# A fused WKV attention and mixture-of-experts kernel: fixed places for expert 0's weight parts, another order of loads and tables in the head, finer routing steps in the transition

## The chip, the core and the metric

The kernel runs on one NeuronCore of a Trainium2 chip. The core has TensorE (PE; its weight loads are listed as PEld), VectorE (DVE), ScalarE (ACT), GpSimd (POOL) and SyncE (SP, which here only issues DMAs). Each engine works through its own instructions in the order in which they were written, and semaphores make it wait for the others. The metric is the device time of one execution in microseconds.

## What is computed

Two layers follow one another. The first is a linear attention (WKV) over `r, k, v` of shape (4, 8, 768, 48), with one decay `w` and one bonus `u` per head and dimension:

```python
for t in range(S):
    kt, vt, rt = (k[:, :, t], v[:, :, t], r[:, :, t])
    cur = np.einsum('bhd,bhe->bhde', u[None] * kt, vt)
    y[:, :, t] = np.einsum('bhd,bhde->bhe', rt, state + cur)
    state = w[None, :, :, None] * state + np.einsum('bhd,bhe->bhde', kt, vt)
```

Its output, as 3072 tokens of 384 numbers, goes into a mixture of eight experts with a noisy top-2 router:

```python
logits = x @ w_gate
noisy_logits = logits + np.log1p(np.exp(x @ w_noise)) * noise
top2 = np.argpartition(-noisy_logits, 2, axis=1)[:, :2]
# softmax over the two, then for each expert e and each of its tokens:
h = np.maximum(x[mask] @ w1[e], 0.0)      # 384 -> 1024
out[mask] += top2_w[mask, k, None] * (h @ w2[e])   # 1024 -> 384
```

All inputs and the output are float32. The expert products are made from two fp32r parts of each operand, a high part and the low rest, with three matmuls for one (high by high, high by low, low by high).

## The kernel before

The schedule is written out by hand: the order of the Python calls is the order of each engine's instructions.

**Head.** SP issues the loads of the first chunks of `k`, `r`, `v`, then `u`, the gate's weights and the noise. DVE and ACT build tables of powers of the decay: `pwk` and `pwr` (lines 160 to 177), `w128` (line 179). PE turns `pwk` around, and ACT copies the result into `tabk` (line 194), by which every later chunk of `k` is multiplied on POOL (`prep_k`, line 307). POOL also makes the products `r*k*u` (`uterm_a`, lines 314 and 316); `uterm_b` sums them on DVE and scales `v` by them (`cv`).

**Attention.** 24 chunks of 128 tokens (`NT`; six time steps for each of four batches). Iteration i of the loop transposes chunk i+1 (`trans`), turns chunk i-1's output for the gate (`xtrans`), updates the state (`zup`: DVE `zt`, ACT `z` and `zb`), makes `cv` of chunk i+1 (`uterm_b`, on DVE up to chunk 8, on ACT in eight pieces from chunk 9 on), computes the output of chunk i on PE (`yout`) and adds `cv` on DVE (`xout`, `x`, line 404), makes the gate's logits of chunk i-1, then the scores of chunk i+1 (`scores`, PE, line 346), which DVE masks (`mask`, `am`, line 354). The next `yout` needs `am`, and the next `xtrans` needs `x`.

**Routing.** After 8, 16 and 24 chunks a group of chunks is routed: some ninety small DVE instructions and a few PE matmuls into one PSUM bank (`RT`), written as the generator `route`. `rstep(us)` takes as many of its pieces as a credit in microseconds allows, at three places of each iteration. When a piece ends with PE work, `at_pe` and `gap` hold that work back for `gap` calls. `drop` turns slots into lists (one-hot products `r_oa`, `r_ob` on DVE, lines 510 to 519, then eight matmuls, line 523).

**Expert weights.** An expert has seven weight units (three of `w1`, four of `w2`, named `w0h/w0l` and `w1h/w1l` on chip). Each unit is a generator: SP loads it into one of three staging buffers (`stg`, line 276), then after `NLAG` empty steps ACT copies the high part (line 279), then DVE subtracts it for the low part (line 281). `wstep()` moves every running unit by one step and starts the next when fewer than three run. Expert 0's units run inside the attention loop, before `yout`, by two `wstep` calls in each iteration from 2 to 10 and one afterwards.

**Transition.** Expert 0's tokens come in three chunks, (0,0), (0,1), (0,2), of two, two and two and a half tiles. `p1` makes the hidden layer: 8 groups f of 9 matmuls, ACT and DVE write the two parts `hb` (and `ht` for the half tile), with three PSUM buffers in turn. `p2` makes the output: 24 matmuls for each tile. While these run, DVE finishes group 2's routing and the lists for all experts (`rest`, by `rest_step`), POOL gathers rows (`xg`), `xT` turns them (PE `ptm`, ACT `xh`, DVE `xl`), and expert 1's weights are split. From chunk (1,0) on the work is the same for each expert.

## Time and profile before

| | |
|---|---|
| Median of 3 runs | 660.09 us (659.82 to 660.27) |
| The profiled execution | 659.12 us, its span 657.4 us |
| PE busy | 626.2 us (95%) |
| DVE busy | 349.4 us (53%) |
| ACT busy | 262.7 us (40%) |
| POOL busy | 262.9 us (40%) |
| HBM read and written | 59.03 MB and 19.76 MB |

A row of a timeline gives start, duration, engine, source line, operation, tiles and a count; in brackets stands the idle time of that engine just before, and what ended it. Times are microseconds from the start of the span. Matmuls overlap one another in the pipeline, so PE is idle only where no matmul is under way. In the rows of a window, each engine's busy time is followed by its count of instructions; PEclk is the share of full TensorE speed that was granted.

### The profile page before, as it was taken

How to read it: one execution, taken by the hardware profiler on the slowest of the kernel's cores; microseconds unless marked ns; L12 is line 12 of the kernel's file. 1: busy time of each engine (PE TensorE's matmuls, PEld its weight loads, DVE VectorE, ACT ScalarE, POOL GpSimd, SP SyncE). 2: the span in 40 equal slices, each digit the busy share in tenths (PEclk: the TensorE clock that was granted, in tenths of full speed). 3: DMA queues.
4: the chain of work that ended last, by engine and by line, in shares of the span. 5: the costliest groups of instructions: out<-in, count | busy, mean ns of one | idle time of the engine just before them, and what ended most of it. 6: DMA issues, size and time to landing. Idle time of an engine off the chain costs nothing.

```text
span 657.4 us, 11894 instructions
## 1 busy us (share of the span) xinstructions
PE 626.2 (95%) x4436; PEld 595.4 (91%) x4437; DVE 349.4 (53%) x883; ACT 262.7 (40%) x737; POOL 262.9 (40%) x389
## 2 busy tenths in 40 slices
PE   7999889999997889999999999999999999999993
PEld 4998789998897879999999999999999999999993
DVE  8786778797479935253452525345252534523230
ACT  1566656775323424243251524325152433523210
POOL 8775526453101247313631641363174136315211
PEclk9999979999999999999999999999999999999997
DMA  8997667773204535242533434253343425302101
GB/s 128 233 227 175 133 142 164 162 174 101 81 1 153 184 118 167 90 133 74 182 107 104 152 98 134 71 183 100 111 153 96 132 72 181 95 26 86 37 2 37
DMA packets 111444, 78.87 MB, mean 120 GB/s; under 512 B 86721, under 2 KB 101441, under 8 KB 111378
## 3 DMA queue, kind: packets, MB, share of 16 engines
q1 hardware_dynamic: 101442, 49.19, 30.2%
q0 software_dynamic: 9936, 28.83, 14.0%
q8 instruction: 37, 0.61, 0.4%
q14 instruction: 29, 0.24, 0.1%
HBM read 59.03 MB, written 19.76 MB: 120 GB/s over the span
## 4 chain that ended last, share of the span: by engine, by line
PE 83%; DVE 11%; ACT 2%; issue 2%; DMA 0%; POOL 0%; POOLq 0%; DVEq 0%; SPq 0%
PE ph L857 31%; PE pym L891 30%; PE py L396 5%; PE pa L346 3%; PE ptm L832 3%; DVE am L354 2%; PE pl L426 2%; PE py L388 2%; PE pym L884 2%; PE pt L334 2%; PE pym L882 2%; PE pwarm L364 1%; DVE RT L454 1%; PE ptx L414 1%; ACT cv L327 1%
## 5 line engine op out<-in xcount | busy, mean ns | idle before, releaser
L891 PE MATMUL pym<-w1h,hb 128*128 128x384 f32 x768 | 204.2, 339 | 0.0
L912 POOL DMA_INDIRECT out_dram<-ot,TK x56 | 57.6, 1029 | 219.9 <-DVE ot L908 200.6
L857 PE MATMUL ph<-xh,w0h 128*128 128x384 f32 (+3 forms) x408 | 142.3, 349 | 1.7 <-ACT xh L833 1.7
L891 PEld LDWEIGHTS pym<-w1h,hb 128*128 128x128 f32 x768 | 139.4, 188 | 1.1 <-issue 0.3
L857 PE MATMUL ph<-xl,w0h 128*128 128x384 f32 (+3 forms) x408 | 139.6, 342 | 0.5 <-DVE xl L834 0.2
L857 PE MATMUL ph<-xh,w0l 128*128 128x384 f32 (+3 forms) x408 | 139.4, 342 | 0.0
L861 DVE SCALAR_TENSOR_TENSOR hb<-ph,hb 128x384 fp32r<-128x384 f32 (+1 forms) x136 | 72.4, 532 | 113.9 <-ACT ht L859 68.4
L891 PE MATMUL pym<-w1l,hb 128*128 128x384 f32 x384 | 129.3, 337 | 0.0
L859 ACT ACTIVATE hb<-ph 128x384 fp32r<-128x384 f32 (+1 forms) x136 | 64.3, 473 | 120.0 <-PE ph L857 112.4
L897 ACT ACTIVATE ot<-pym 128x384 f32<-128x384 f32 x45 | 22.1, 492 | 160.4 <-PE pym L891 155.8
L805 POOL DMA_INDIRECT xg<-xd,GR x56 | 54.0, 964 | 80.1 <-DVE f L687 35.1
L857 PEld LDWEIGHTS ph<-xh,w0h 128*128 128x128 f32 x408 | 77.1, 189 | 5.1 <-ACT xh L833 2.4
L857 PEld LDWEIGHTS ph<-xl,w0h 128*128 128x128 f32 x408 | 77.1, 189 | 3.7 <-DVE xl L834 1.2
L857 PEld LDWEIGHTS ph<-xh,w0l 128*128 128x128 f32 x408 | 77.2, 189 | 2.6
L891 PEld LDWEIGHTS pym<-w1l,hb 128*128 128x128 f32 x384 | 72.2, 188 | 0.1
L834 DVE TENSOR_TENSOR xl<-ptm,xh 128x384 fp32r<-128x384 f32 (+1 forms) x56 | 28.9, 524 | 74.3 <-ACT xh L833 63.3
L814 POOL DMA_INDIRECT pv<-out_dram,GA x49 | 55.6, 1134 | 25.9 <-issue 14.9
L396 PE MATMUL py<-vt,am 128*128 128x96 f32 x384 | 60.8, 284 | 2.9 <-DVE am L354 2.0
L396 PEld LDWEIGHTS py<-vt,am 128*128 128x128 f32 x384 | 52.0, 197 | 5.1 <-DVE am L354 4.8
L307 POOL TENSOR_TENSOR kd<-kt,tabk 128x192 f32<-128x192 f32 x46 | 27.4, 617 | 57.8 <-PE pwarm L364 50.6
L281 DVE TENSOR_TENSOR w1l<-stg,w1h 128x768 fp32r<-128x768 f32 x32 | 30.8, 961 | 10.2 <-ACT w1h L279 10.2
L354 DVE TENSOR_TENSOR am<-pa,mneg 128x512 int32<-128x512 int32 x48 | 30.7, 680 | 8.8 <-PE pa L346 6.9
(205 smaller groups left out, 865.8 us busy)
## 6 DMA issues: line engine op xcount, KB each, us to landing
stg<-in_moe_w_dram SPq DMA_DIRECT2D x24, 512.0 KB, 4.2
stg<-in_moe_w_dram SPq DMA_DIRECT2D x32, 384.0 KB, 3.3
rd<-in_r_dram SPq DMA_DIRECT2D x24, 192.0 KB, 4.5
vt<-in_v_dram SPq DMA_DIRECT2D x24, 192.0 KB, 4.1
xd<-x SPq DMA_DIRECT2D x24, 192.0 KB, 2.0
out_dram<-zrow SPq DMA_DIRECT2D x16, 288.0 KB, 3.7
kt<-in_k_dram SPq DMA_DIRECT2D x23, 192.0 KB, 3.3
xg<-xd,GR POOLq DMA_INDIRECT x56
```

The lines of the kernel that those rows point to most:

```text
L281: nc.vector.tensor_sub(lo, tv, hi.bitcast(F32))
L307: (eng or nc.gpsimd).tensor_mul(kd[i % 3][:, h, :D], kt[i][:, h], tabk[:, h, :D])
L354: nc.vector.tensor_tensor(am[:, s].bitcast(I32), pa[s].bitcast(I32), mneg.to_broadcast([128, NP, 128]), op=ALU.bitwise_and)
L396: nc.tensor.matmul(o2, AM[i][:, s, p, :], vt[i][:, h, None, :].to_broadcast([128, 2, D]), start=not c and h == 0, stop=h == H - 1, skip_gr ...
L805: nc.gpsimd.indirect_dma_start(out=xg[:n], out_offset=None, in_=xd[:GROUPS[GEARLY - 1][1] * 128] if early_ else xd, in_offset=bass.Indirec ...
L814: nc.gpsimd.indirect_dma_start(out=pv[:n], out_offset=None, in_=out, in_offset=bass.IndirectOffsetOnAxis(ap=GA[:n, e * NJ + t:e * NJ + t + ...
L834: nc.vector.tensor_sub(xl[:, :, o:o + n], pt[:, :, :n], xh[:, :, o:o + n].bitcast(F32))
L857: nc.tensor.matmul(ph[:, :w_], a[:, d, fs], x[:, d, :w_], start=(j == 0), stop=(j == len(q) - 1))
L859: nc.scalar.activation(h_[:, f, 0, :], ph[:, a:b], AF.Relu)
L861: nc.vector.scalar_tensor_tensor(h_[:, f, 1, :], ph[:, a:b], 0.0, h_[:, f, 0, :].bitcast(F32), op0=ALU.max, op1=ALU.subtract)
L891: nc.tensor.matmul(py, hb[:, f, a, hs], x[:, f, :], start=(j == 0), stop=(j == len(q) - 1))
L912: st = nc.gpsimd.indirect_dma_start(out=out, out_offset=bass.IndirectOffsetOnAxis(ap=TK[:n, q:q + 1], axis=0), in_=ot[:n], in_offset=None, ...
```

## The change

Three groups of edits.

**Expert 0's weights.** `wstep` leaves the attention loop. Three tables say in which iteration each of the seven units is loaded (`W_LD`), copied (`W_HI`) and subtracted (`W_LO`). The copy stays where `wstep` was; the subtraction and the load go to the end of the iteration, behind `mask` and `kvup`. Units 5 and 6 wait in their staging buffers for iterations 21 and 22.

**Head.** Chunk 1's `k` and chunk 0's `v` are loaded ahead of `u`, chunk 1's `r` after them. Half of `pwr` is copied by ACT rather than DVE, `w128` is made after the first transposed tiles. POOL prepares chunk 1 of `k` before chunk 0's products. DVE's preparation of chunk 0 (`prep_k(0)`, `uterm_b(0)`) goes behind the transposes of chunk 1, thus behind `rT` of chunk 1.

**Transition.** Routing steps run between the matmuls of `p2(0,0)`, at every eighth, with a third of the credit. `gap` stays 2 in the rest of the lists, with slightly larger credits. Expert 1's weight steps are left out of `p1(0,2)` and doubled in `p1(1,0)`. The first tile of chunk (1,0) is turned inside `p2(0,2)`, one tile ahead.

```diff
+W_LD = {1: (0,), 2: (1, 2), 4: (3,), 5: (4,), 6: (5,), 7: (6,)}
+W_HI = {4: (0,), 5: (1,), 6: (2,), 7: (3,), 8: (4,), 21: (5,), 22: (6,)}
+W_LO = {4: (0,), 5: (1,), 6: (2,), 7: (3,), 8: (4,), 22: (5,)}
...
     load(0, (0, 2))
+    load(1, (0, 1))
+    load(0, (2, 3))
+    load(1, (1, 2))
     ub = const.tile([128, H, D], F32, name="ub")
     nc.sync.dma_start(ub, ...)
-    load(0, (2, 3))
-    load(1)
+    load(1, (2, 3))
...
-    nc.vector.tensor_copy(pwr[:, :, 0:64], pwk[:, :, 127:63:-1])
+    nc.scalar.activation(pwr[:, :, 0:64], pwk[:, :, 127:63:-1], AF.Copy)
...
-    NLAG = [4]
+    NLAG = [1]
...
-    wq.extend(w_split(0))
+    wun = w_split(0)
     consts_a()
+    prep_k(1)
     uterm_a(0)
-    prep_k(1)
     uterm_a(1)
     consts_b()
     scores(0)
     mask(0)
-    prep_k(0, nc.vector)
-    uterm_b(0)
...
             trans(i + 1)
+        if i == 0:
+            prep_k(0, nc.vector)
+            uterm_b(0)
...
-        for _ in range(0 if i < 2 else 2 if i < 11 else 1):
-            wstep()
+        for p in W_HI.get(i, ()):
+            next(wun[p])
...
         kvup(i)
         rstep(STEPS_KV)
+        for p in W_LO.get(i, ()) + W_LD.get(i, ()):
+            next(wun[p])
...
-    while wq or wrun:
-        wstep()
+    next(wun[6])
...
-    for t in p2(0, 0):
-        rstep(STEPS_P2)
+    for t in p2(0, 0, lambda: rstep(STEPS_P2 / 3)):
...
-    gap[0] = 1
-    for t in p2(0, 1, lambda: rest_step(1.0)):
+    for t in p2(0, 1, lambda: rest_step(1.2)):
...
             if s == 2:
-                rest_step(STEPS_P1)
-            elif XT_AT <= j < XT_AT + 2:
+                rest_step(1.1)
+                continue
+            if XT_AT <= j < XT_AT + 2:
                 next(xt, None)
             wstep()
+            if s == 3:
+                wstep()
...
-            if s > 2:
+            if s > 2 or listed[0] and t > chunks(e)[ci][0]:
                 next(xt, None)
```

Where instructions move, three places matter. The first is DVE around the attention's iteration 8, where group 0's routing begins (`x` and `am` belong to the loop, `w1l` is a weight's low part, the rest is routing). Before:

```order
L321 TENSOR_REDUCE c_979<-rku 128x8
L281 TENSOR_TENSOR w1l_720<-stg,w1h_719 128x768 x2
L404 TENSOR_TENSOR x<-py,cv 128x384
L354 TENSOR_TENSOR am<-pa,mneg 128x512 x2
L565 SCALAR_TENSOR_TENSOR RT<-lg 128x64
L567 TENSOR_SCALAR r_a<-RT 128x64
```

Now:

```order
L327 TENSOR_REDUCE c_980<-rku 128x8
L410 TENSOR_TENSOR x<-py,cv 128x384
L360 TENSOR_TENSOR am<-pa,mneg 128x512 x2
L571 SCALAR_TENSOR_TENSOR RT<-lg 128x64
L573 TENSOR_SCALAR r_a<-RT 128x64
L574 SCALAR_TENSOR_TENSOR RT<-lg,nz 128x64
L448 TENSOR_SCALAR RT<-r_a 128x64
L450 TENSOR_SCALAR RT<-RT 128x64
L578 TENSOR_TENSOR r_zp<-RT,lg 128x64
L287 TENSOR_TENSOR w1l_673<-stg,w1h_672 128x768
L345 TENSOR_TENSOR rT<-pt,pwr 128x512
```

The two low parts ahead of `x` are gone from there; one comes behind `am` and the first routing pieces, ahead of the next `rT`.

The second place is DVE in `p1(0,2)`, between the first and the last list of group 2 (`hb` and `ht` empty PE's hidden groups, `r_oa` and `r_ob` are what PE's list matmuls wait for). Before:

```order
L514 TENSOR_TENSOR r_ob<-r_ej,ij 128x8x49
L281 TENSOR_TENSOR w1l_3181<-stg,w1h_3180 128x768
L861 SCALAR_TENSOR_TENSOR hb<-ph,hb 128x256
L861 SCALAR_TENSOR_TENSOR ht<-ph,ht 128x64
L517 TENSOR_TENSOR r_ob<-r_ob,thi 128x8x49
L281 TENSOR_TENSOR w1l_3181<-stg,w1h_3180 128x768
L861 SCALAR_TENSOR_TENSOR hb<-ph,hb 128x256
L861 SCALAR_TENSOR_TENSOR ht<-ph,ht 128x64
L519 TENSOR_SCALAR r_ob<-r_ob,pcol 128x8x49
```

Now:

```order
L520 TENSOR_TENSOR r_ob<-r_ej,ij 128x8x49
L523 TENSOR_TENSOR r_ob<-r_ob,thi 128x8x49
L867 SCALAR_TENSOR_TENSOR hb<-ph,hb 128x256
L867 SCALAR_TENSOR_TENSOR ht<-ph,ht 128x64
L525 TENSOR_SCALAR r_ob<-r_ob,pcol 128x8x49
```

The weight parts between the pieces of `r_ob` have left; they come in `p2(0,2)` and `p1(1,0)`.

The third place is ACT from the end of `p2(0,2)` into `p1(1,0)`, where expert 1's and expert 2's high parts are copied. Before:

```order
L886 ACTIVATE ot<-pym 64x384
L833 ACTIVATE xh<-ptm 128x3x128
L835 ACTIVATE GT<-xg 128x1
L833 ACTIVATE xh<-ptm 128x3x128
L835 ACTIVATE GT<-xg 128x1
L833 ACTIVATE xh<-ptm 128x3x128
L835 ACTIVATE GT<-xg 128x1
L859 ACTIVATE hb<-ph 128x384 x4
L279 ACTIVATE w0h_3550<-stg 128x1024
L859 ACTIVATE hb<-ph 128x384
```

Now:

```order
L892 ACTIVATE ot<-pym 64x384
L839 ACTIVATE xh<-ptm 128x3x128
L841 ACTIVATE GT<-xg 128x1
L285 ACTIVATE w1h_3180<-stg 128x768
L839 ACTIVATE xh<-ptm 128x3x128
L841 ACTIVATE GT<-xg 128x1
L865 ACTIVATE hb<-ph 128x384
L285 ACTIVATE w1h_3180<-stg 128x768
L865 ACTIVATE hb<-ph 128x384
L285 ACTIVATE w1h_3180<-stg 128x768
L865 ACTIVATE hb<-ph 128x384
L285 ACTIVATE w0h_3548<-stg 128x1024 x2
```

One of the three `xh` has moved ahead of `ot`; three copies of expert 1 and two of expert 2 now stand between the first `hb`.

More of the change, by code (lines that the diff above doesn't have):

```diff
@@ L176 @@
     nc.vector.tensor_mul(pwk[:, :, 96:128], pwk[:, :, 64:96], pwk[:, :, 95:96].to_broadcast([128, NP, 32]))
-    nc.vector.tensor_copy(pwr[:, :, 0:64], pwk[:, :, 127:63:-1])
+    nc.scalar.activation(pwr[:, :, 0:64], pwk[:, :, 127:63:-1], AF.Copy)
     w128 = const.tile([128, NP, 1], F32, name="w128")
-    nc.vector.tensor_mul(w128, tmpw[:, :, 63:64], tmpw[:, :, 63:64])
     kT, rT = {}, {}
@@ L194 @@
     nc.scalar.activation(tabk.rearrange("p h d -> p (h d)"), ptab.rearrange("p a b -> p (a b)"), AF.Copy)
+    nc.vector.tensor_mul(w128, tmpw[:, :, 63:64], tmpw[:, :, 63:64])
     acc = const.tile([128, E], BF16, name="acc")
```

## The prediction

> **What bounds the kernel now.** First the chain of waits by engine, then the stages, cut where a chunk's scores start.
>
> ```profile
> PE 83%; DVE 11%; ACT 2%; issue 2%; DMA 0%; POOL 0%; POOLq 0%; DVEq 0%; SPq 0%
> ```
>
> ```profile
> 0.00:14.46 14.46, 10.28 (x64) 6.24 (x65) 12.44 (x29) 3.21 (x6) 11.78 (x42) 1.00 0.87 139
> 14.46:62.34 47.88, 47.80 (x560) 45.41 (x561) 38.10 (x63) 28.29 (x80) 33.26 (x53) 1.00 0.96 203
> 62.34:90.88 28.54, 23.26 (x220) 21.07 (x219) 19.66 (x73) 16.79 (x59) 11.55 (x18) 0.88 0.64 143
> 90.88:163.80 72.92, 71.10 (x815) 67.09 (x814) 59.63 (x196) 49.35 (x175) 37.01 (x62) 1.00 0.67 151
> 163.80:242.61 78.81, 69.36 (x516) 65.76 (x515) 56.16 (x212) 25.76 (x71) 14.77 (x22) 1.00 0.34 105
> 242.61:657.40 414.79, 404.35 (x2266) 389.87 (x2266) 163.39 (x314) 139.24 (x349) 154.51 (x195) 0.99 0.34 105
> ```
>
> (Columns: window, length, busy time of PE, PEld, DVE, ACT, POOL, granted clock, DMA share, GB/s.) From 242.61 on, PE is busy but for 10.44 of 415 us, and the change touches only the first hidden layer there. PE is idle for 4.18 us in the head, 5.28 us in chunks 9 to 11 (with a clock of 0.88), and 9.45 us in the transition. Those three are what the change can earn.
>
> Why chunks 9 to 11 stall is in the timeline:
>
> ```profile
> 61.58 1.91 ACT L327 ACTIVATE cv<-vt,c 128x48 f32<-128x48 f32 x8
> 64.25 1.06 DVE L281 TENSOR_TENSOR w1l<-stg,w1h 128x768 fp32r<-128x768 f32 x1 [2.98 <-ACT w1h L279]
> 65.93 0.52 PE L414 MATMUL ptx<-ident,x 128*128 128x128 f32 x3 [0.91 <-DVE x L404]
> 70.11 0.38 PE L346 MATMUL pa<-rT,kT 64*128 64x128 f32 x2
> 80.53 0.96 DVE L281 TENSOR_TENSOR w1l<-stg,w1h 128x768 fp32r<-128x768 f32 x1 [4.05 <-ACT w1h L279]
> 83.68 0.87 PE L414 MATMUL ptx<-ident,x 128*128 128x128 f32 x3 [3.12 <-DVE RT L591]
> ```
>
> DVE stood 2.98 and 4.05 us before a low part, because ACT copies the high part only after the eight pieces of `cv`; `x`, `am` and the routing pieces were queued behind it, and PE's `ptx` waited for `x`. The second gap also cost clock:
>
> ```profile
> 79.90:83.31 3.41, 0.67 (x7) 0.43 (x4) 2.61 (x9) 1.14 (x3) 3.41 (x6) 1.00 0.00 0
> 83.31:90.14 6.83, 6.26 (x28) 5.96 (x28) 4.75 (x29) 3.52 (x13) 0.27 (x1) 0.50 0.76 162
> 223.26:226.67 3.41, 2.00 (x19) 2.00 (x19) 3.41 (x10) 0.08 (x1) 0.00 (x0) 1.00 0.82 226
> 240.32:243.74 3.42, 1.53 (x7) 1.03 (x8) 2.71 (x6) 1.39 (x6) 1.99 (x2) 1.00 0.16 58
> 243.74:247.15 3.41, 3.41 (x13) 3.41 (x12) 0.56 (x1) 0.49 (x1) 2.69 (x3) 0.50 0.54 140
> ```
>
> Half clock followed stretches of 3.41 us with 0.67 and 1.53 us of PE work, and none followed 2.00 us. A half-clock stretch of 3.41 us costs up to 1.7.
>
> **Part 1: chunks 9 to 11.** What routing alone costs is seen in group 1, which has the same pieces and no weight work. I lay its chunks 17 to 19 over 9 to 11:
>
> ```profile
> 123.99:143.43 19.44, 19.31 (x220) 18.10 (x219) 17.31 (x69) 12.65 (x46) 10.08 (x18) 1.00 0.75 164
> 130.25 0.38 PE L346 MATMUL pa<-rT,kT 64*128 64x128 f32 x2
> 132.82 1.22 DVE L354 TENSOR_TENSOR am<-pa,mneg 128x512 int32<-128x512 int32 x2
> 137.17 0.38 PE L346 MATMUL pa<-rT,kT 64*128 64x128 f32 x2
> 143.43 0.38 PE L346 MATMUL pa<-rT,kT 64*128 64x128 f32 x2
> ```
>
> An unhindered chunk takes 143.43 - 137.17 = 6.26; the one before took 6.92, since `am` came 2.57 us after the scores had started. Now one low part (0.96, the row at 80.53) is left in this stretch, unit 4's, behind the first routing pieces. DVE is busy 17.31 of 19.44 us there, so I charge it in full: 19.44 + 0.96 = 20.40 against 28.54, **8.1 us** gained, the dip included. Bounds: 28.54 - 3 x 6.26 = 9.8 if DVE absorbs everything; 5.5 if the 0.96 is paid twice and the later `am` brings a dip of 1.7.
>
> Chunks 4 to 8 lose to DVE here only by little: 47.88 - 47.80 leaves 0.1 us of PE idle over nine chunks. With `x` ahead of the low part I take **0.3**, from 0 to 0.5. The price is on SP: from iteration 4 a stage load waits at the iteration's end for the low part behind `am`, and `kt`, `rd`, `vt` of a later chunk and the store of `x` are queued behind it. That is some 4 us after the scores started (1.2 for them, 1.2 for `am`, and the low part, which I put at 1.5 as it has a third more columns than the 0.96 row). Medians from issue to landing:
>
> ```profile
> kt<-in_k_dram SPq DMA_DIRECT2D x23, 192.0 KB, 3.3
> stg<-in_moe_w_dram SPq DMA_DIRECT2D x24, 512.0 KB, 4.2
> ```
>
> So POOL prepares a chunk about 1 us late, and PE transposes it some 4 us after that. Hidden; the cover is POOL's idle time (47.88 - 33.26 = 14.6 us here). The two last units, moved to iterations 21 and 22 (two copies on ACT, two low parts on DVE), fall into waits for PE and cost nothing; without that cover 2 x 0.96.
>
> **Part 2: the head.**
>
> ```profile
> 6.10 1.34 POOL L314 TENSOR_TENSOR rku<-rd,kd 128x192 f32<-128x192 f32 x2 [0.95 <-DMA rd<-in_r_dram]
> 6.42 0.57 DVE L177 COPY pwr<-stg 128x256 f32<-128x256 f32 x1
> 7.20 0.60 ACT L194 ACTIVATE tabk<-ptab 128x512 f32<-128x512 f32 x1 [1.23 <-PE ptab L192]
> 7.38 0.68 DVE L187 TENSOR_TENSOR kT<-pt,stg 128x512 f32<-128x512 f32 x1
> 8.07 1.18 POOL L316 TENSOR_TENSOR rku<-rku,ub 128x192 f32<-128x192 f32 x2 [0.63 <-DMA ub<-in_u_dram]
> 9.72 1.14 POOL L307 TENSOR_TENSOR kd<-kt,tabk 128x192 f32<-128x192 f32 x2 [0.47 <-DMA kt<-in_k_dram]
> 16.11 1.27 DVE L354 TENSOR_TENSOR am<-pa,mneg 128x512 int32<-128x512 int32 x2
> ```
>
> DVE's `kT` starts when the tables end (6.4), not at 7.38, so the first scores come 0.96 earlier. But POOL now begins with `kd`, which needs `tabk`, ready at 7.80, where it had the first product done by 7.44. POOL's chain from there is `kd` 1.14 and four product pairs of 1.2 to 1.3, to 14.1, against 13.3 before; DVE needs it for chunk 1's sum, then makes `cv` and `x` and comes to `am` at 15.85, not 16.11. I take **0.3**: bounds +1.0 (the whole 0.96) and -0.5 (`u` is loaded behind three more loads, and POOL waited 0.63 for it already).
>
> **Part 3: the transition.**
>
> ```profile
> 200.22 0.35 PE L523 MATMUL RT<-r_ob,r_oa 128*128 128x14 bf16 x8 [1.11 <-DVE r_ob L519]
> 207.79 0.51 PE L523 MATMUL RT<-r_ob,r_oa 128*128 128x98 bf16 x8 [1.15 <-DVE r_ob L519]
> 222.96 0.95 DVE L281 TENSOR_TENSOR w1l<-stg,w1h 128x768 fp32r<-128x768 f32 x1
> 224.66 0.51 PE L523 MATMUL RT<-r_ob,r_oa 128*128 128x98 bf16 x8 [2.55 <-DVE r_ob L519]
> 239.57 0.49 ACT L886 ACTIVATE ot<-pym 64x384 f32<-64x384 f32 x1 [2.28 <-PE pym L884]
> 241.49 0.55 PE L832 MATMUL ptm<-ident,xg 128*128 128x128 f32 x3 [1.30 <-DVE xl L834]
> 242.61 0.45 PE L857 MATMUL ph<-xh,w0h 128*128 128x384 f32 x1 [0.58 <-ACT xh L833]
> 246.27 0.56 DVE L861 SCALAR_TENSOR_TENSOR hb<-ph,hb 128x384 fp32r<-128x384 f32 x1 [2.54 <-ACT hb L859]
> ```
>
> - Finer steps in `p2(0,0)` bring group 2's first PE work ahead of `p1(0,1)`; DVE's chain starts about 2.4 us earlier, and the first list comes behind seven hidden groups. Gap 1.11 and some of the smaller ones behind it: 1.6.
> - Gap 1.15 gets a call more. That gives 0.9 on PE, but DVE is full here, and the next `xl` comes no earlier than DVE's chain allows: nothing further.
> - Gap 2.55: the three low parts on DVE (0.95 each) leave. By DVE's chain 0.8 remains, 0.45 for a buffer and 0.4 for `r_ob`: 1.75.
> - At the end, one of three tiles is turned ahead of the half tile. But a high part (0.85) now stands on ACT between the second and third `xh`, and a low part (0.95) on DVE between the second and third `xl`. From the end of the half tile's matmuls (239.5) the layer now flows after 3.1 us, and fully about 0.6 later, when the last `xl` is there. By the same durations I get 2.4 and 3.5: 0, and the stretch of little PE work stays.
> - New: `p1(1,0)` takes two weight steps for each group. Expert 2's loads wait for staging buffers that expert 1's low parts, now behind the first `hb`, hold until about 7 us after 239.5 (flow from 3.5, a group of 1.4, `hb` 0.5 and 0.56, a low part 0.95). They land 3.3 to 4.2 us later, the second after the first; ACT has two copies ahead of the fourth `hb` and waits for them until about 12, then copies for 1 us, while the seventh group needs that `hb`'s buffer at 12.7. The stall is 1.5 to 2.0. The present half clock (1.7) and it hide each other: whichever comes, the layer takes what it takes now. Cost 0 if only one comes, 1.7 if both, gain 1.7 if neither.
>
> Sum 1.6 + 1.75 = 3.35, taken as **3.4**; bounds 0 and 5.4.
>
> [...]
>
> **Sum.** 8.1 + 0.3 + 0.3 + 3.4 = 12.1 us off the profiled execution's own 659.12 gives 647.0. The median of the runs, 660.09, stands 0.97 above it, so **648.0 us** is predicted.
>
> **The rivals.**
>
> 1. *Everything is hidden.* DVE absorbs its low part (+1.7), the head gives its full 0.96 (+0.7), neither stall nor dip in `p1(1,0)` (+1.7): 648.0 - 4.1 = 643.9. For it: DVE has 2.1 us free in group 1's three chunks. Against: its idle time there lies before routing begins.
> 2. *The transition gives its gain back.* DVE is its bound from 200 to 230, and stall and dip both come in `p1(1,0)`: 648.0 + 3.4 = 651.4. For it: DVE's share between 163.80 and 242.61 and the doubled steps; against: three low parts do leave DVE.
> 3. *The change doesn't do what it says.* Not the low part but ACT's `cv` with routing on DVE makes chunks 9 to 11 slow; only the dip and its gap go, and three chunks stay at 7.77 (62.34 to 70.11): 28.54 - 23.31 = 5.2 instead of 8.1, 650.9. Against: group 1 has both and runs at 6.48 a chunk.
> 4. *Slower: SP starves the chunks.* A stage load that waits for a low part holds the loads behind it, while the DMA share is 0.96 in chunks 2 to 8. It decides once a chunk's `kt` lands more than about 4 us later than I work out, that is, once POOL's slack is gone; then each of iterations 3 to 8 waits. At 2.1 us each, six cost the whole gain; at 2.5 the time is 648.0 + 15 = 663. Against: the bytes are the same, and the loads are made two iterations ahead.
>
> **How the numbers follow.** Forecast 0.58, rival 1 0.11, rival 2 0.16, rival 3 0.09, rival 4 0.06. The range, 643.5 to 652.5, takes in rivals 1 to 3 and the bounds of part 1, leaving out most of rival 4 and the far ends of sums of bounds. Faster by over 0.2% (about what a measurement tells from no change, 1.3 us): all but rival 4, 0.94; rival 4 is split into 0.02 within 0.2% and 0.04 slower.
>
> **What would show it.** In the changed profile chunk 9 takes 6.3, chunk 10 about 7.9 and chunk 11 6.3 us, no low part waits for ACT there, and the clock stays at 1.00 from 62 to 165. The second `am` starts near 15.9. The three list gaps fall from 4.8 to about 1 us in sum. In `p1(1,0)` ACT waits for a stage load ahead of `w0h`, or the clock is halved. The prediction is wrong if PE waits for `kT` or `rT` in chunks 4 to 8, if chunks 9 to 11 take over 23 us, or if the transition is not at least 2 us shorter.

## The result, and the profile after

| | before | changed |
|---|---|---|
| Median of 3 runs | 660.09 us (659.82 to 660.27) | 650.66 us (648.81 to 651.46) |
| The profiled execution | 659.12 us, span 657.4 | 650.66 us, span 648.8 |

The ratio is 0.9851, with a 95% interval of 0.9823 to 0.9879: 9.8 us less, between 8.0 and 11.7. The predicted time was 648.0 us, in a range of 643.5 to 652.5. A second session, with five executions of the unaltered changed kernel beside eight of the kernel before, gave 649.77 against 661.98 us: 0.9821 (0.9798 to 0.9844), 11.8 us less.

The chain of waits of the first profile can be followed back only to about 164 us, so its shares can't be laid beside those of before. That of the second profile, which goes back to the head, has 8% of DVE instead of 11%:

```profile
PE 85%; DVE 8%; DMA 2%; ACT 1%; issue 1%; POOL 1%; SPq 1%; POOLq 0%; DVEq 0%
```

The stages of the first profile, cut at the same events as those of before (columns as there):

```profile
0.00:13.82 13.82, 11.99 (x63) 7.77 (x65) 7.71 (x25) 3.63 (x7) 9.26 (x38) 1.00 0.90 143
13.82:63.17 49.35, 48.60 (x561) 45.38 (x560) 38.74 (x66) 27.12 (x76) 37.27 (x57) 1.00 0.95 196
63.17:83.66 20.49, 19.46 (x220) 18.09 (x219) 18.18 (x70) 14.82 (x53) 10.82 (x18) 1.00 0.93 201
83.66:156.58 72.92, 71.09 (x814) 67.10 (x814) 59.57 (x198) 52.06 (x185) 36.95 (x62) 1.00 0.67 152
156.58:231.16 74.58, 70.22 (x516) 66.96 (x515) 55.20 (x209) 24.40 (x70) 13.26 (x20) 0.98 0.27 85
231.16:648.80 417.64, 404.42 (x2266) 389.63 (x2266) 165.96 (x319) 140.50 (x351) 155.62 (x196) 0.99 0.35 109
```

Chunks 9 to 11 fell from 28.54 to 20.49 us, and their clock rose from 0.88 to 1.00. The 72.92 us behind them are unchanged to the hundredth. The transition up to expert 1's first hidden layer fell from 78.81 to 74.58. Two stages became longer: the first two together by 0.83 us (62.34 to 63.17), and the last by 2.85 (414.79 to 417.64).

Chunks 10 and 11 in the timeline of the changed kernel, first PE, then DVE and ACT:

```profile
69.52 1.16 PE L352 MATMUL pa<-rT,kT 64*128 64x128 f32 x16
73.10 0.55 PE L420 MATMUL ptx<-ident,x 128*128 128x128 f32 x3 [0.90 <-ACT lg L434]
77.40 1.16 PE L352 MATMUL pa<-rT,kT 64*128 64x128 f32 x16
```

```profile
67.20 1.18 DVE L287 TENSOR_TENSOR w1l<-stg,w1h 128x768 fp32r<-128x768 f32 x1
73.06 1.22 DVE L360 TENSOR_TENSOR am<-pa,mneg 128x512 int32<-128x512 int32 x2
71.06 1.91 ACT L333 ACTIVATE cv<-vt,c 128x48 f32<-128x48 f32 x8
72.88 0.16 ACT L434 ACTIVATE lg<-pl 128x16 f32<-128x16 f32 x1
```

The one low part left in this stretch waits for nobody, and the three chunks take 6.35, 7.88 and 6.26 us. Chunk 10 is the long one: `am` starts 3.54 us after its scores, where in chunk 18 of the kernel before it was 2.57, and PE's `ptx` waits 0.90 us for `lg`, which stands behind the eight pieces of `cv` on ACT. (`ptx` and `pl` share a PSUM buffer, which `lg` empties.)

The transition, PE rows with idle time ahead of them, and the wait of ACT for a stage load:

```profile
202.26 0.41 PE L863 MATMUL ph<-xh,w0h 128*128 128x320 f32 x1 [0.76 <-ACT xh L839]
203.69 0.41 PE L863 MATMUL ph<-xl,w0h 128*128 128x320 f32 x1 [1.02 <-DVE xl L840]
231.16 0.44 PE L863 MATMUL ph<-xh,w0h 128*128 128x384 f32 x1 [1.64 <-ACT xh L839]
232.21 0.69 PE L863 MATMUL ph<-xl,w0h 128*128 128x384 f32 x1 [0.61 <-DVE xl L840]
245.81 0.44 PE L863 MATMUL ph<-xh,w0h 128*128 128x384 f32 x1 [2.12 <-DVE hb L867]
```

```profile
241.72 1.06 ACT L285 ACTIVATE w0h<-stg 128x1024 fp32r<-128x1024 f32 x1 [2.84 <-DMA stg<-in_moe_w_dram]
```

The list gaps of 1.11, 1.15 and 2.55 us are gone. New are 1.02 us of waiting for `xl`, which stands behind list pieces on DVE, and the stall of 2.12 us ahead of the seventh group of expert 1's first hidden layer. ACT waited 2.84 us for expert 2's first load and 0.96 us for its second, so the `hb` behind them came late. The two stretches with idle time were followed by half clock:

```profile
201.08:204.49 3.41, 1.63 (x10) 1.25 (x10) 3.34 (x7) 2.14 (x7) 0.00 (x0) 1.00 0.28 95
204.49:207.90 3.41, 3.41 (x16) 3.21 (x15) 3.21 (x8) 0.50 (x2) 0.63 (x1) 0.50 0.42 131
228.39:231.80 3.41, 1.57 (x10) 1.00 (x8) 2.38 (x5) 2.27 (x6) 0.56 (x2) 1.00 0.16 58
231.80:235.21 3.41, 3.00 (x9) 3.00 (x10) 0.67 (x2) 0.04 (x1) 2.63 (x3) 0.50 0.62 190
```

The head lost time where a gain had been forecast. Its rows in the changed profile, and the third scores of before for comparison:

```profile
5.36 1.08 PE L190 MATMUL pt<-ident,kd 128*128 128x128 f32 x4 [0.52 <-POOL thi L246]
9.23 1.48 PE L352 MATMUL pa<-rT,kT 64*128 64x128 f32 x16
20.95 1.16 PE L352 MATMUL pa<-rT,kT 64*128 64x128 f32 x16
```

```profile
19.84 1.16 PE L346 MATMUL pa<-rT,kT 64*128 64x128 f32 x16
```

Four transposes that took 0.63 us before took 1.08 here, and the first scores 1.48 instead of 1.16: the full clock came only at 9.93 us, in the profile of before at 4.80. Stage by stage (the second profile of the changed kernel is that of an experiment below; "last scores" are those of chunk 23):

| From ... to | before | changed | changed, second profile | predicted change |
|---|---|---|---|---|
| start ... third scores | 19.84 | 20.95 | 19.93 | -0.3 |
| ... scores of chunk 9 | 42.50 | 42.22 | 42.57 | -0.3 |
| ... scores of chunk 12 | 28.54 | 20.49 | 20.71 | -8.1 |
| ... last scores | 72.92 | 72.92 | 72.74 | 0 |
| ... expert 0's first hidden layer | 7.81 | 7.05 | 7.69 | 0 |
| ... second layer of (1,0) | 86.27 | 85.46 | 83.34 | -3.4 |
| ... end of the span | 399.52 | 399.71 | 399.62 | 0 |
| span | 657.40 | 648.80 | 646.60 | -12.1 |

### The profile page after: what moved, and what is told of

Same layout as the page of the kernel before. It is cut to its first block, busy times and chain, and to the rows that moved or that the text cites. A ratio compares the mean times of both kernels' runs of the same rounds, so it can differ in the third digit from the quotient of the medians.

```text
span 648.8 us, 11891 instructions
## 1 busy us (share of the span) xinstructions
PE 625.8 (96%) x4436; PEld 594.9 (92%) x4437; DVE 345.3 (53%) x882; ACT 262.5 (40%) x738; POOL 263.2 (41%) x389
## 3 DMA queue, kind: packets, MB, share of 16 engines
q0 software_dynamic: 9936, 28.83, 14.1%
## 4 chain that ended last, share of the span: by engine, by line
PE 69%; DVE 3%; DMA 1%; ACT 1%; issue 0%; POOL 0%; POOLq 0%
PE ph L863 33%; PE pym L897 30%; PE ptm L838 2%; PE pym L890 2%; PE pym L888 2%; DMA stg<-in_moe_w_dram 1%; DVE xl L840 0%; DVE w1l L287 0%; DVE r_oa L516 0%; PE py L402 0%; ACT hb L865 0%; DVE hb L867 0%; PE pl L432 0%; PE RT L529 0%; DVE w0l L287 0%
## 5 line engine op out<-in xcount | busy, mean ns | idle before, releaser
L402 PE MATMUL py<-vt,am 128*128 128x96 f32 x384 | 58.8, 278 | 1.9 <-DVE am L360 0.8
L402 PEld LDWEIGHTS py<-vt,am 128*128 128x128 f32 x384 | 50.2, 192 | 4.1 <-DVE am L360 3.7
L313 POOL TENSOR_TENSOR kd<-kt,tabk 128x192 f32<-128x192 f32 x46 | 29.0, 652 | 51.6 <-PE pwarm L370 34.8
L360 DVE TENSOR_TENSOR am<-pa,mneg 128x512 int32<-128x512 int32 x48 | 30.7, 681 | 14.3 <-PE pa L352 14.2
L914 DVE SCALAR_TENSOR_TENSOR ot<-ot,GT,pv 128x384 f32<-128x384 f32 (+1 forms) x46 | 27.0, 610 | 11.0 <-ACT ot L903 11.0
```

The lines of the kernel that those rows point to most:

```text
L313: (eng or nc.gpsimd).tensor_mul(kd[i % 3][:, h, :D], kt[i][:, h], tabk[:, h, :D])
L360: nc.vector.tensor_tensor(am[:, s].bitcast(I32), pa[s].bitcast(I32), mneg.to_broadcast([128, NP, 128]), op=ALU.bitwise_and)
L402: nc.tensor.matmul(o2, AM[i][:, s, p, :], vt[i][:, h, None, :].to_broadcast([128, 2, D]), start=not c and h == 0, stop=h == H - 1, skip_gr ...
L914: nc.vector.scalar_tensor_tensor(ot[:n], pt[:n], g, PV[e, t][:n], op0=ALU.mult, op1=ALU.add)
```

## The experiments

Two questions were open: why the head lost 1.1 us, and where the 3.4 us of the transition had gone. Theory A held that the head's loss came from the clock of that execution; the rival, that the new order itself was slower.

### Each part alone on the kernel before

Each of three kernels has one part of the change, the other two undone. The first keeps `W_LD`, `W_HI`, `W_LO` and their calls, the second the loads, tables and POOL order of the head, the third the edits from `p2(0, 0, ...)` on.

> The kernel before with one part of the change alone: the fixed places of expert 0's weight parts. Head and transition are as before. Theory A (the parts add up; this part gives what the changed profile shows between the scores of chunk 4 and of chunk 12): chunks 9 to 11 take 20.5 us instead of 28.5, chunks 4 to 8 0.3 less, so 660.1 - 8.3 = 651.8 us (651.0 to 652.6). Theory B (part of the 8.1 us comes from the head's new order, because chunks that reach POOL and DVE in another phase stall less): chunks 9 to 11 stay above 22 us and the time is 653.5 or more.

> The kernel before with the head's part alone: order of loads, the table copy on ACT, the chunk-1 product ahead on POOL. Theory A (clock): the 1.1 us that the changed head lost came from a full clock granted only at 9.93 us instead of 4.80, which doubled the transposes, the warm matmuls and half of the first scores; the order itself is worth -0.5. Then the third scores start at 19.2 to 19.6 where the full clock comes by about 5 us, near 20.9 where it comes near 10, and in between otherwise; the median is 659.3 to 661.2 and the single times spread by up to 1.7 us. Theory B (order): POOL's chain, which now begins with the product that needs the table, sets DVE's second mask, whatever the clock: the third scores start at 20.6 or later also with an early full clock, and the median is 661.2.

> The kernel before with the transition's part alone. Theory A (the parts add up): from the last scores to the second layer of expert 1's first chunk 92.5 us, as in the changed kernel, instead of 94.1; the list gaps (1.1, 1.2 and 2.6 us) are gone, and a stall of about 2 us ahead of the seventh group of expert 1's first hidden layer takes part of it back: 660.1 - 1.6 = 658.5 us, with 1.7 more or less for each half-clock stretch that is there or not. Theory B (the finer steps need the free DVE that the moved weight parts leave): 94 us or more, and 660 us.

| | median | before beside it | ratio | difference, us |
|---|---|---|---|---|
| weight places alone | 653.67 (6 runs) | 661.61 (23 runs) | 0.9868 (0.9833 to 0.9904) | -8.7 (-11.0 to -6.4) |
| head alone | 660.60 (12 runs) | 661.61 | 0.9988 (0.9970 to 1.0007) | -0.8 (-2.0 to +0.5) |
| transition alone | 659.58 (12 runs) | 661.61 | 0.9973 (0.9948 to 0.9997) | -1.8 (-3.4 to -0.2) |

(The differences are the ratios by 661.61.) They add up to 11.3 us, and the whole change gave 11.8 in the second session: within intervals of some 2 us either way, the parts do not lean on one another. By its numbers the run of the weight places came out as theory B had it (chunks 9 to 11 above 22 us, a time above 653.5). But the kernel before was slower beside it too, and the gain of 8.7 us is theory A's 8.3. Chunks 9 to 11 in the kernel with the weight places alone:

```profile
64.34:86.84 22.50, 21.24 (x221) 19.72 (x220) 18.40 (x70) 15.48 (x55) 10.79 (x18) 0.92 0.86 185
73.38:76.79 3.41, 2.21 (x17) 1.79 (x16) 3.27 (x10) 2.17 (x9) 2.42 (x5) 1.00 0.74 170
```

Chunk 10's wait ahead of `ptx` was 1.07 us there instead of 0.90, and the window behind the second row ran at half clock. That is the dip that stood in the prediction's lower bound for this part. That the head's order made these chunks short (theory B) is ruled out by a kernel further below, the changed one without its head edit: they take 20.62 us there, at full clock. The head alone moved the median by nothing that can be told from zero. Its third scores started at 20.86 with the full clock from 10.08: the value that both theories allowed, so this run does not separate them. The transition alone took 92.34 us from the last scores to the second layer of (1,0), which is theory A's 92.5, not theory B's 94; two stretches of half clock lay in it.

### A longer warm-up

```diff
-WARM0 = 8
+WARM0 = 10
```

> The changed kernel with ten warm matmuls at the start instead of eight, so that PE is busy without a gap from 1.24 us into the transposes (the changed profile has 0.52 us of idle there, and the full clock came only 5 us later). Theory A (clock): the full clock is granted by 8.1 us at the latest in every execution, the third scores start at 19.3 to 20.2 instead of 20.95, and the time is 649.0 to 650.0 with less spread. Theory B (order of the head): the third scores stay at 20.9 or come 0.3 later because of the longer warm-up, and the time is 650.7 to 651.0.

650.01 us (6 runs, 647.56 to 653.95). The full clock came at 6.3 us and the first two scores at 7.91 and 12.18 instead of 9.23 and 13.82. The third still started at 21.61 (timeline, then windows):

```profile
15.54 0.44 PE L340 MATMUL pt<-ident,kd 128*128 128x128 f32 x2 [1.71 <-POOL kd L313]
```

```profile
13.10:16.51 3.41, 1.27 (x25) 0.79 (x22) 2.35 (x5) 0.00 (x0) 3.41 (x7) 1.00 0.70 54
16.51:19.92 3.41, 3.41 (x17) 3.41 (x18) 2.83 (x5) 1.85 (x6) 2.67 (x5) 0.50 1.10 175
```

Theory A's start of 19.3 to 20.2 us did not come. With an early clock PE runs ahead and then waits 1.71 us for POOL's `kd` of chunk 2, and in this execution the 3.41 us from 16.51 on ran at half clock. The spread did not shrink either.

### The changed kernel again

> The changed kernel once more, unaltered, as the reference for the variants beside it and for a second profile of it. Theory A (the half-clock stretches follow free-running windows of 3.41 us; the same idle time of PE halves the clock or not, depending on how the windows lie in that execution): the single times spread over 3 us or more and fall with the granted clock, with a median of 650.0 to 651.5; in the profile the idle times at the start of expert 0's last and expert 1's first hidden layer are the same as in the first profile (0.76 and 1.02, 1.64 and 0.61 us), but the stretches of half clock need not be there. Theory B (each of these idle times halves the clock by itself): both stretches are there again at the same places, and the times agree within 1 us.

649.77 us (5 runs, 648.38 to 650.31), at a granted clock of 0.989 to 0.994; the spread was 1.9 us instead of the 3 expected, and the median lay just under the 650.0 to 651.5 of theory A. This profile has the clock at 1.00 from 4.2 us to the end of the work:

```profile
15.45 0.44 PE L340 MATMUL pt<-ident,kd 128*128 128x128 f32 x2 [1.69 <-POOL kd L313]
16.20 1.27 DVE L360 TENSOR_TENSOR am<-pa,mneg 128x512 int32<-128x512 int32 x2
19.93 1.16 PE L352 MATMUL pa<-rT,kT 64*128 64x128 f32 x16
203.74 0.41 PE L863 MATMUL ph<-xl,w0h 128*128 128x320 f32 x1 [1.02 <-DVE xl L840]
```

```profile
198.80:202.22 3.42, 2.75 (x25) 2.40 (x21) 3.35 (x7) 1.62 (x8) 0.00 (x0) 1.00 0.37 110
202.22:205.63 3.41, 2.30 (x14) 2.08 (x15) 3.41 (x6) 1.46 (x5) 0.00 (x0) 1.00 0.03 9
163.64:246.98 83.34, 76.40 (x535) 73.12 (x536) 62.52 (x220) 30.70 (x79) 20.88 (x26) 1.00 0.33 103
```

The wait of 1.02 us is the same as in the first profile. There it lay in one window with the 0.76 us ahead of it, which left 1.63 us of PE work, and half clock followed. Here the border of two windows, counted in steps of 3.41 us from the clock's rise at 4.2 us, falls between the two waits, 2.75 and 2.30 us of work remain, and the clock stays. So theory B is out: the same waits were followed by half clock in one execution and not in the other. Theory A's reason, the place of the windows, fits this pair, but PE's work in a window does not decide alone: a window of the first profile kept the full clock with only 1.66 us of work, at the stall ahead of the seventh group,

```profile
242.04:245.45 3.41, 1.66 (x11) 1.38 (x9) 1.48 (x2) 2.45 (x5) 0.97 (x1) 1.00 0.56 181
```

and two of the second profile did with 1.89 and 1.87.

The price of a stretch of half clock can also be read. From expert 0's first hidden layer to the second layer of (1,0), in the kernel before (one such stretch), in the kernel with the head alone, whose transition is that of before (none), and in the first profile of the changed kernel (two):

```profile
171.61:257.88 86.27, 78.07 (x535) 74.83 (x536) 61.24 (x219) 30.67 (x78) 23.98 (x30) 0.98 0.34 104
```

```profile
172.83:257.51 84.68, 76.48 (x535) 73.31 (x536) 61.65 (x221) 30.94 (x79) 22.69 (x29) 1.00 0.34 103
```

```profile
163.63:249.09 85.46, 79.00 (x535) 75.78 (x536) 62.56 (x220) 30.74 (x79) 21.79 (x28) 0.96 0.33 104
```

PE's busy time is 76.40 and 76.48 us without a stretch, 78.07 with one and 79.00 with two: 1.3 to 1.7 us each. In the layers' length they cost 0.8 us (14.58 against 13.82, expert 0's last) and 1.4 to 1.6 (17.93 against 16.53, and 15.27 against 13.70 with the transition of before, expert 1's first).

The stall ahead of the seventh group differs too. The kernel with the longer warm-up has the same transition and lost no clock in it, but its stall was 0.55 us instead of 2.07:

```profile
164.93:246.70 81.77, 76.34 (x536) 73.06 (x536) 62.50 (x220) 30.85 (x79) 19.76 (x25) 1.00 0.33 105
```

So the changed transition takes 81.77 or 83.34 us at full clock, that of before 84.68.

At an early clock the new head brings the third scores at 19.93, the old one at 19.84.

### POOL's old order in the head

```diff
-WARM0 = 8
+WARM0 = 10
...
     load(0, (0, 2))
+    ub = const.tile(...)      # u loaded here, not behind three more loads
     load(1, (0, 1))
...
     consts_a()
-    prep_k(1)
     uterm_a(0)
+    prep_k(1)
     uterm_a(1)
```

> The changed kernel with ten warm matmuls, and with POOL's old order in the head: the product of chunk 0 first, while the tables are made, u loaded before chunk 1. Theory A (chunk 2's product stands at the end of POOL's chain, which the change lets begin only when the table is there): that product is done by 15.3 us instead of 16.35, PE does not wait 1.7 us for it, no half clock follows there, and the third scores start at 19.2 to 20.0, against 21.62 with ten warm matmuls and POOL's new order; median 648.0 to 649.3. Theory B (DVE's full queue from the first mask to the second sets the third scores): they start at 20.7 or later, and the median stays at 650.

648.58 us (5 runs, 648.40 to 650.72). In the timeline:

```profile
11.61 0.69 DVE L345 TENSOR_TENSOR rT<-pt,pwr 128x512 f32<-128x512 f32 x1 [1.52 <-PE pt L340]
13.55 1.45 POOL L313 TENSOR_TENSOR kd<-kt,tabk 128x192 f32<-128x192 f32 x2
16.36 1.27 DVE L360 TENSOR_TENSOR am<-pa,mneg 128x512 int32<-128x512 int32 x2
```

POOL's `kd` of chunk 2 is done at 15.0 as expected, and PE does not wait for it. But now `kd` of chunk 1 is late, DVE waits 1.52 us for the transposes that follow it, and the second `am` starts at 16.36 instead of 16.20. Neither theory named this. The two orders exchange one wait for another of the same length, and the third scores start at 20.09, within 0.2 us. The median is 1.2 us below that of the unaltered kernel, with ranges that overlap; what is behind that was not settled.

### The changed kernel without its head edit

> The changed kernel with the whole head edit undone. Theory A (the new head exchanges one limit for another: the second mask starts at 16.1 to 16.4 us in both orders, so that the order is worth 0.3 at most): median within 0.8 of the unaltered kernel's 649.8; third scores at 19.8 to 20.0 where the full clock comes by 5 us and is not lost, 20.7 or later where half clock follows the head's idle time. Theory B (the new head costs 1.1 us, as the first pair of profiles reads): median 648.7 or less. Theory C (the new head is worth 0.8 to 1.0, as the comparison of the head alone could be read): median 650.6 or more.

648.93 us (6 runs, 647.01 to 653.07). This run, the next one and the last one (all of it together) were made in a third session, in which the kernel before had a median of 660.79 us instead of 661.98. So they are compared with the unaltered changed kernel by the ratio to the kernel before beside each: 0.9830 (0.9791 to 0.9870) here, 0.9821 (0.9798 to 0.9844) there. These intervals decide nothing among the three theories. The third scores decide for A: 20.01 with an early full clock (four transposes into `ptab` took 0.63 us at 6.91 us, where in the first changed profile, ahead of its full clock, they took 1.06), beside 19.93 with the new order. Together with the head alone (-0.8, -2.0 to +0.5) the order is worth nothing that can be told from zero.

### Weight steps: one instead of two in expert 1's first hidden layer

```diff
             if s == 2:
                 rest_step(1.1)
-                continue
-            if XT_AT <= j < XT_AT + 2:
+            elif XT_AT <= j < XT_AT + 2:
                 next(xt, None)
             wstep()
-            if s == 3:
-                wstep()
```

> The changed kernel with one edit of the transition undone: a weight step for each group of expert 0's last hidden layer again, and one instead of two in expert 1's first; the larger routing allowance (1.1) stays. Theory A (the list gap of 2.55 us ahead of the last list came from the three low parts on DVE among the list pieces; and the stall ahead of the seventh group comes from the steps that were moved behind it): a gap of 1.5 us or more is back ahead of the last list, expert 1's first hidden layer has no gap ahead of its seventh group and takes 13.6 to 14.2 us, 1.7 more with half clock; the two about cancel, median 649.3 to 650.8 beside 649.8 for the unaltered kernel. Theory B (the allowance closed the list gap, not the moved low parts): the gap stays under 0.8 us, the stall is gone all the same, and the median is 648.0 to 648.8.

647.90 us (6 runs, 647.27 to 649.99), a ratio of 0.9819 (0.9787 to 0.9851) to the kernel before, where the unaltered changed kernel had 0.9821. The rows of PE with idle time, then the stretch from expert 0's first hidden layer to the second layer of (1,0):

```profile
213.67 0.51 PE L529 MATMUL RT<-r_ob,r_oa 128*128 128x98 bf16 x8 [1.00 <-DVE r_ob L525]
219.47 0.51 PE L529 MATMUL RT<-r_ob,r_oa 128*128 128x98 bf16 x8 [1.21 <-DVE r_ob L525]
231.66 0.44 PE L863 MATMUL ph<-xh,w0h 128*128 128x384 f32 x1 [0.91 <-ACT xh L839]
```

```profile
163.40:245.68 82.28, 76.18 (x536) 73.16 (x536) 62.49 (x222) 30.98 (x79) 21.65 (x27) 1.00 0.34 103
```

Theory A's mechanism holds in the main: list gaps of 1.00 and 1.21 us are back, 2.2 in sum, there is no stall, and the layer takes 14.02 us. (The gap ahead of the last list, 1.21, is less than the 1.5 that A named and more than the 0.8 of B.) Whether the two cancel, the profiles leave open: at the same clock (1.00) this stretch takes 82.28 us with the edit undone, and 83.34 (second profile) or 81.77 (longer warm-up) with it. Against the second profile: expert 0's last chunk is 1.5 us longer without the edit (0.9 in the hidden layer; 0.6 in the second layer up to the next chunk's start, where 0.91 us of idle time instead of 1.64 gives back part of the 1.21), expert 1's first hidden layer 2.5 us shorter (14.02 against 16.53). That would make moving the weight steps 1.0 us dearer than leaving them, but the kernel with the longer warm-up turns the sign, and the two ratios are equal.

### Weight steps within expert 0's last second layer

```diff
-        for t in p2(e, ci, (lambda: rest_step(1.0)) if s == 2 else None):
+        def lstep():
+            rest_step(1.0)
+            if listed[0]:
+                wstep()
+
+        for t in p2(e, ci, lstep if s == 2 else None):
```

> The changed kernel with the last weight steps of expert 1 called within expert 0's last second layer, once its lists are done, instead of in the hidden layer behind it. Theory A (the stall ahead of the seventh group, 0.55 to 2.12 us in the profiles so far, is ACT waiting for stage loads that wait for staging buffers held by low parts behind the first group): no wait of ACT for a stage load there, no gap ahead of the seventh group, and the 1.64 us at the layer's start shrink by about the 0.85 us of the high part that stood between the second and third tile; the layer takes 13.8 to 14.4 us without a half-clock stretch and 15.5 to 16.0 with one; median 1.5 to 2.5 below the unaltered kernel. Theory B (the stage loads are late because the DMA engines are busy, not because of the buffers): the gap stays at 0.5 us or more.

646.90 us (5 runs, 645.69 to 648.30), 2.9 below the unaltered kernel beside it (649.77, 648.38 to 650.31). ACT, then PE, then the same stretch as above:

```profile
225.98 0.85 ACT L285 ACTIVATE w1h<-stg 128x768 fp32r<-128x768 f32 x1 [2.96 <-DMA stg<-in_moe_w_dram]
235.17 1.05 ACT L285 ACTIVATE w0h<-stg 128x1024 fp32r<-128x1024 f32 x1
```

```profile
230.66 0.45 PE L863 MATMUL ph<-xh,w0h 128*128 128x384 f32 x1 [0.58 <-ACT xh L839]
```

```profile
164.49:244.63 80.14, 76.33 (x535) 73.07 (x536) 63.86 (x222) 30.85 (x79) 21.11 (x26) 1.00 0.36 114
```

Theory A holds: expert 2's copies wait for no load, the seventh group is on time, the layer starts after 0.58 us instead of 1.64, and takes 13.97 us. The load that ACT still waits for (2.96 us) is expert 1's last, at a place where nobody waits for ACT. The stretch is 3.2 us shorter than in the unaltered kernel at the same clock (83.34), and 1.6 shorter than with the longer warm-up (81.77). So the buffers are what holds these loads back; why the same loads then end in stalls of 0.55 to 2.58 us (the latter in the kernel with POOL's old order) is not shown.

### Matmuls of no use in the idle time

Eight and ten matmuls of 512 columns on a free PSUM buffer, ahead of expert 0's last and expert 1's first hidden layer.

> The changed kernel with eight and ten matmuls of no use (512 columns, about 0.21 us each) ahead of expert 0's last and expert 1's first hidden layer, where PE is idle for 0.76 + 1.02 and 1.64 + 0.61 us. They delay nothing by more than 0.2 us if PE is really idle there. Theory A (too little PE work in a 3.41 us window halves the clock for the next): the clock stays at 1.00 from 195 to 240 us in every execution; a median 0.5 to 2.0 below the unaltered kernel and 3.4 below its first profile's account; the remaining spread is the head's and that of the stall ahead of the seventh group. Theory B (the clock is lowered by something other than idle time of PE, such as the restart itself): the stretches stay and the time is the same or 0.3 longer.

649.37 us (5 runs, 648.07 to 651.45). The clock from the layer's start to the next second layer:

```profile
197.50:250.22 52.72, 49.24 (x316) 44.78 (x314) 37.90 (x94) 21.99 (x54) 19.29 (x24) 1.00 0.41 126
```

It stayed at 1.00, but so it did in the second profile of the unaltered kernel, and 0.4 us between the medians is less than their spread. This neither supports nor refutes the effect. In this execution chunk 10 had its wait ahead of `ptx`, here 1.32 us, in one window, and the window behind it ran at half clock:

```profile
71.98:75.39 3.41, 1.95 (x15) 1.49 (x13) 3.24 (x11) 2.80 (x11) 2.79 (x6) 1.00 0.62 135
```

### All of it together

POOL's old order with ten warm matmuls, the steps within the second layer, eight and five matmuls of no use.

> The changed kernel with ten warm matmuls and POOL's old order in the head, the last weight steps of expert 1 within expert 0's last second layer, and eight and five matmuls of no use ahead of the two hidden layers that begin with idle time. Theory A (stall and half-clock stretches are what the transition still loses, and both are removed): no wait of ACT for a stage load in expert 1's first hidden layer, that layer 13.5 to 14.2 us, a clock of 1.00 from 90 us to the end of the work, a median of 645.0 to 646.5, below the 646.9 of the moved steps alone, and a spread of the single times under 2.5 us, what remains being the head and chunk 10. Theory B (the matmuls of no use delay the layers as much as they save): 647 to 648.

644.81 us (6 runs, 643.98 to 645.67), 0.9765 (0.9734 to 0.9797) of the kernel before, whose 11 runs beside it had a median of 660.79. The unaltered changed kernel had 0.9821 of it and the moved steps alone 0.9775 (0.9749 to 0.9801), so it is faster than the first by some 3.7 us and can't be told from the second. Its times spread over 1.7 us. Its stretch from expert 0's first hidden layer:

```profile
163.21:244.04 80.83, 78.40 (x546) 74.16 (x549) 63.92 (x222) 30.90 (x79) 21.25 (x26) 1.00 0.36 114
```

That is 0.7 us more than in the profile of the moved steps alone, so the matmuls of no use may delay the layers a little where the clock would not have been lost, as theory B says; two profiles do not show it. The median lies just below theory A's range (645.0 to 646.5), but expert 1's first hidden layer took 14.47 us, not 13.5 to 14.2. What each of the parts adds these runs do not tell.

## Why the prediction came out as it did

**Chunks 9 to 11 (8.1 us): right, for the reason given.** 28.54 became 20.49, forecast 20.40. The chunks took 6.35, 7.88 and 6.26 us, forecast 6.3, 7.9 and 6.3; no low part waits for ACT; the weight places alone are worth 8.7 us (6.4 to 11.0). Rival 3, that `cv` with routing keeps all three slow, is out; only in chunk 10 does PE wait behind `cv`, 0.90 us for `lg`. The 7.88 us of that chunk are 0.96 more than chunk 18's 6.92, the price put on the low part, which itself took 1.18. That no dip came was in part luck: in two of the ten profiles with the new weight places (weight places alone, and the matmuls of no use) this wait, at 1.07 and 1.32 us, was followed by half clock.

**Chunks 4 to 8 (0.3 us): not shown.** From the scores of chunk 4 to those of chunk 9, the first profile has 31.49 us and the second 31.84, against 31.77 before. PE waits there neither for `kT` nor for `rT`, so rival 4, that SP starves the chunks, is out.

**The head (+0.3 us): the sign failed in the first profile, at -1.1, beyond the bound of -0.5.** At an equal clock it is -0.1 (19.84 to 19.93). Two steps failed. The sum took PE's durations of the old head as given, while the clock in the head differs from execution to execution (full from 9.93 us in the first profile of the changed kernel, from 4.2 in the second). And POOL's chain was followed only to the product pairs (14.1), not to `kd` of chunk 2 behind them, for which PE waits 1.7 us. The second `am`, forecast for 15.85, started at 17.22 with the late clock and at 16.20 with the early one.

**The transition (3.4 us): 0.8 in the first profile, 2.9 in the second** (86.27 to 85.46 and 83.34). The prediction named a transition less than 2 us shorter as a sign of being wrong: the first profile shows it, the second does not. The lists came out as forecast or better: no gap over 0.3 us is left of the 4.8, and the wait that was said to take the place of the 1.15 is the 1.02 us for `xl`. From expert 0's first to the start of expert 1's first hidden layer the two profiles are 3.5 and 4.2 us shorter than before, forecast 3.35, although half clock came at expert 0's last layer in the first, which the prediction did not have.

The step that failed is the last one, the cost of the doubled steps in expert 1's first hidden layer. Stall and half clock were said to hide each other there, at no cost if only one came and 1.7 us if both. With both (first profile) the layer took 17.93 us against 15.27, 2.7 more; with the stall alone it took 16.53 in the second profile, 1.3 more. The stall, put at 1.5 to 2.0, was 2.12 and 2.07 us there, and the half clock that it was to replace is worth less: 1.6 of that layer (15.27 before, 13.70 with the head alone, where the clock stayed). The start of the layer, put at no net cost, has 0.4 us more idle time (2.25 against 1.88). Nor has the stall one size: it was 0.55 with the longer warm-up, where the layer took 15.00, a little less than before. At full clock, against 84.68 us, the transition as changed gains 1.3 to 2.9 us, without the moved steps 2.4, and with them in the second layer 4.5; each is a difference of single profiles.

**Sum.** The forecast took 12.1 us off the profiled execution; 8.5 came off in the first profile (659.12 to 650.66), and 11.8 by the ratio of the second session, which is near the forecast though the head gave nothing and the transition's last step was off: later executions of the kernel before were granted less clock (0.982 on average) than the one from which the sum started (0.987). That profile was one of its quicker executions (659.12 us): later medians of the same kernel were 661.61, 661.98 and 660.79. The first median, 650.66, lies nearer to rival 2's 651.4 than to the forecast, and stall and dip of rival 2 were both in its profile; but the lists kept their gain, so DVE did not bound the transition up to there as rival 2 had it.

## What to carry to other kernels

A queue that is emptied faster hands the wait to the next thing in order: before weight steps are moved behind a stage, look at which staging buffers they keep and which loads wait for those buffers. The idle time of an engine that nobody waits for (ACT and DVE in expert 0's last second layer) is the place for such steps, and there the kernel was 2.9 us faster than with the steps behind it. And a single profile of a kernel with short stretches of idle TensorE has a luck of its own in the clock (spans of 648.80 and 646.60 us for the same kernel, with two stretches of half clock and none): two profiles, or the granted clock of each run, should stand behind any term below 2 us.

## What was not expected of the hardware

The same program loses clock in some executions and not in others: five executions of the unaltered changed kernel were granted 0.989 to 0.994 of the full clock. The changes of the clock lie whole steps of 3.41 us apart: from 204.49 to 231.80 in the changed profile are 27.31 us, 8.00 such steps. These steps do not lie at the same times in different executions: counted back to the start of the span, one begins at 3.11 us in the changed profile, and at 1.39 in that of before. The clock fell after windows of one step with 1.27, 1.57, 1.63, 1.95 and 2.21 us of PE work, and stayed after 2.30 and 2.75, but also after 1.66, 1.87 and 1.89, and after 2.00 (a row of the prediction). So between about 1.6 and 2.2 us the same amount of work goes with either outcome, and what decides there is not shown. In the rows above, the full clock came back after windows with 3.00 us of PE work or more, and in the head of the changed kernel not after this one, but after the next, with 3.41:

```profile
3.11:6.52 3.41, 2.82 (x10) 1.06 (x7) 2.16 (x8) 1.13 (x3) 2.13 (x11) 1.00 1.19 194
```

(The clock column reads 1.00 ahead of the first recorded change, at 9.93 us, though four transposes took 1.08 us there, against 0.63 in the profile of before.) The kernel before was hit more often: its runs beside the experiments had a mean granted clock of 0.982 to 0.984, those of the changed kernel 0.991. In the profile of before 6.83 us of half clock, from 83.31 to 90.14, stand around the end of PE's wait of 3.12 us in chunk 11 and behind it; both profiles of the unaltered changed kernel have full clock throughout these chunks. So a part of the 11.8 us that the change saves is clock that is no longer lost there.
